# Chunked linear attention and a gated MLP: scores, state and previous output in one tensor-engine visit, a one-sided bounds pass, weight words checked on a second load

## The chip, the cores and the metric

One core of a Trainium2 chip runs one program. The engines are TensorE (PE; its weight loads are PEld), VectorE (DVE), ScalarE (ACT), GpSimd (POOL) and SyncE (SP, which here only issues DMAs). The metric is device time in microseconds. Three executions of the kernel before took 359.44, 359.44 and 360.03 us, median 359.44.

## The reference

Shapes: r, k, v, w are (4 batches, 8 heads, 768 steps, 48), float32; u is (8, 48). The weights are float64 in memory: w_in 384x1024, conv_w 3x1024, w_out 1024x384.

```
state = zeros(B, H, 48, 48)
for t in range(768):
    cur = outer(u * k_t, v_t)
    y_t = r_t @ (state + cur)
    state = w_t[:, None] * state + outer(k_t, v_t)
x = y, heads side by side                  # (4, 768, 384)
h = relu(x @ w_in)                         # (4, 768, 1024)
c = conv_w[0]*h[t-1] + conv_w[1]*h[t] + conv_w[2]*h[t+1]
out = (h * sigmoid(c)) @ w_out             # (4, 768, 384)
```

w lies between 0.80 and 0.95.

## The kernel before

**Attention, by chunks.** The 4 x 768 steps are N = 24 chunks of L = 128 steps, six to a batch. For a chunk, `loads` brings w, k, r, v in (four DMAs on SP). `stage_a` turns w, k, r so that time lies along the free axis (PE transposes, L610), runs two scans over w on DVE (L619 backwards over the chunk, L627 forwards) and multiplies k and r by them (`kr`). The last column of the backward scan is the decay of the whole chunk. Eight heads of 48 rows are packed as six heads plus 16-row pieces of the other two, and `last` holds the pieces put together: from chunk 4 (`EARLY`) on six small SP DMAs per chunk do that (`spread`, L653). `stage_a` also makes the diagonal term (`pm`, POOL and DVE) and turns k back (`kh`, PE L678). Two ACT passes over the loaded w (`guard`, L686, rank put off by `GUARD`) sum what lies above W_HI = 1.05 and below W_LO = 0.75 into `flags`.

`stage_b(n)` is the part around the change, for chunks from 4 on. It works in 64-row and 64-column pieces of the array. One PE operation, "cross" (L872), does three things: `carried(True)`, the carried state's part in the output of chunk n-1 across the two halves (L819); `scores()` of chunk n (L850); `fresh()`, the growth of the state in chunk n (L860). DVE then merges the scores into `pm` (L875), and adds the growth to the decayed state (`sd`, L704 and L707) for `sa` (L880) and `s` (L887). A DVE memset of one element (`mark`, L892) stands between `cross` and the second PE operation, "output" (L897): `carried(False)` (L819) and `within()` (L829) finish the output of chunk n-1 in the banks `ys` that `cross` began. Both must be ordered with DVE between them, as `output` adds to what `cross` wrote from other row groups. ACT and DVE then split the result into two fp32r parts in `xT` (L904, L906), and every few chunks SP copies pieces of it (L915).

**MLP, by blocks.** Eight blocks of 384 steps. In a block each of the 8 column groups of w_in needs nine 128x128 products of 386 columns, in three operations of three (L926); ACT, DVE and POOL make the gate from them (L938 to L948) into `gh` tiles; then each of 3 row tiles needs 24 products with w_out (L955), ACT copies the sum out (L986) and SP stores it.

**Weights.** float64 words are turned into two fp32r parts by `convert` in 9 + 8 pieces (ACT L498, DVE L500 and L503, POOL L506, ACT L520, POOL L521). The words are in a `raw` tile; `small_words` (L512) is then run on the same tile, two ACT passes that overwrite it and sum into `flags` whether a word is too small for the conversion. `raw` and `gh` tiles share a ring of GH = 5 tiles; a raw tile goes back to the ring when its last reader, `small_words`, has ended. There are six such tiles (three of w_in, three of w_out), and conv_w has a small tile of its own.

**Order.** `Plan.op` records every operation with an engine, a modelled length (`LEN`), what it reads and writes and a rank; `Plan.issue` simulates the engines by these lengths, always starts the ready operation of lowest rank, and the instructions are issued in that order, fixed for each engine. `SHIFT` moves ranks by stage and kind. At the end DVE sums `flags`; if it isn't zero, a slow general program runs after the fast one.

Of the kernel before, what the change touches and what calls it, by code (L numbers as in the profile page):

```python
# [18 lines left out]

W_LO, W_HI = 0.75, 1.05  # L20
BANKS = 8
# [6 lines left out]
SPREAD = (3, 5)  # L28
EARLY = 4
COLD = ((9.9, 1.8), (60.0, 1.3))  # L30
CAPS, KEEPS = (3, 4, 4, 3, 4), (1, 3, 1, 1, 1)
# [6 lines left out]
    tr=0.245, kback=0.245, scores=1.0, carried=0.794, state=0.45, y=0.86, state_y=1.22, mm3=0.529,  # L38
    cross=1.16, ends=0.23, half=0.93, output=0.7, cph=0.35, sa=0.27, xhih=0.29, xloh=0.33,
    scan=0.86, small=0.1, pad=0.07, kt=0.47, dg=0.47, cp=0.62, xlo=0.6, sd=0.22, s=0.27,  # L40
    stt=0.54, gate=0.47, wts=0.47, wstt=0.47,
    fill=0.25, kh=0.42, guard=0.72, sbd=0.34, xhi=0.49, relu=0.5, mul=0.49, sig=0.43, cast=0.42, out=0.37, exp=0.52,
    z=0.98, diag=1.07, lo=0.97,
    words=1.15, fetch=1.5, gather=1.6, rest=0.3, carried_rows=1.4, y_rows=1.5, ones=0.8,
    load=0.55, issue=0.45, spread=0.64,
)
SHAPE = dict(cross=3, ends=3, half=3, output=3, scores=1, state=2, y=2, state_y=2, y_rows=2)
TURN = dict(tr=0.18, kback=0.18, carried=0.18)
PAUSE = 0.08
SHIFT = dict(  # L50
    a5=35, a6=61, a8=98, a10=171, a11=-118, a12=44, a15=22, a16=95, a17=160, a20=-37, a23=35, adg=39, agather=-18,
    aguard=56, akback=-108, akh=8, akt=-485, apad=388, asmall=46, aspread=-166, atr=-9, b1=48, b5=-91, b6=20,
    b7=-165, b8=-169, b9=-43, b10=-82, b13=46, b14=-34, b19=-136, b20=20, b21=-5, b24=-21, bcarried_rows=116,
    bcross=-531, bfill=-210, brest=-34, bs=156, bsa=-12, bscores=152, bsmall=43, bxhih=23, bxloh=-10, i0=-56,
    i1=-16, i2=19, i3=44, i4=-25, i5=-15, i6=-84, imm3=-130, icast=27, igate=14, imul=54, istt=-27, l2=33, l4=54,
    l19=12, l20=-2, o1=58, o2=54, o3=300, o4=-43, o5=-9, omm3=37, oissue=15, p0=150, p1=41, p2=-34, p3=-35, p4=-35,
    p5=-17, p6=64, p7=19, p8=168, p10=97, p12=-670, p14=101, pcast=11, pexp=61, plo=-196, pwords=4,
)
# [79 lines left out]
class Plan:  # L138
# [40 lines left out]
    def issue(self):  # L179
# [34 lines left out]
        while len(order) < n:  # L214
            for e in engines:
                if free[e] > t:
                    continue
                for k, (_, i) in enumerate(sorted(ready[e])):
                    if places(self.ops[i][4]):
                        break  # L220
                else:
                    continue
                ready[e].remove((self.ops[i][7], i))
                _, us, _, _, _, moves, port, _ = self.ops[i]
                at = t
                if e == "PE":
                    us *= next((x for until, x in COLD if t < until), 1.0)
                    at = t + self.turn(before, self.what[i])
                    before = self.what[i]
                if port:  # L230
                    other = "POOL" if e == "DVE" else "DVE"
                    at = max(t, locked[other])
                    locked[e] = at + us
                order.append((at, i))
                free[e] = at + us
                if moves:
                    free[e] += wire.add(e, moves, i, free[e])
                else:
                    heapq.heappush(events, (free[e] + TAIL[e], i))
                heapq.heappush(events, (free[e], -1))  # L240
            t = min(wire.next(), events[0][0] if events else float("inf"))
            assert t < float("inf"), "no order found"
            for i in wire.advance(t):
                heapq.heappush(events, (t + (0.8 if self.ops[i][5][2] == 64 else TAIL["SP"]), i))
            todo = []
            while events and events[0][0] <= t + 1e-9:
                todo.append(heapq.heappop(events)[1])
            for i in todo:
                if i < 0:
                    continue  # L250
                for b in self.ops[i][4]:
                    b.uses -= 1
                    if not b.uses:
                        b.kind.held -= 1
                        b.kind.places.append(b.t)
                for u in users[i]:
                    left[u] -= 1
                    if not left[u]:
                        ready[self.ops[u][0]].append((self.ops[u][7], u))
# [87 lines left out]
def rwkv_conv_moe_kernel(  # L347
# [75 lines left out]
    limits = fconst.tile([P, 8], F32, name="limits")  # L423
    guard_lo, guard_hi, small_lo = limits[:, 0:1], limits[:, 1:2], limits[:, 2:4]
    for j, x in enumerate((W_LO, -W_HI, 0x38200000 * 2.0 ** -30, 0x38200000 * 2.0 ** -30 - 2.0)):
# [7 lines left out]
    flags = fconst.tile([P, N + 7, 2], F32, name="flags")  # L433
    nc.vector.memset(flags[:, N:N + 7, :], 0.0)

# [73 lines left out]
    def small_words(raw, buf, k, n, reads, rows=P):  # L509

        for j, kind in enumerate((U32, I32)):
            op("ACT", "words", lambda j=j, kind=kind: nc.scalar.activation(  # L512
                out=raw()[:, 0:2 * n:2].bitcast(F32), in_=raw()[:, 1:2 * n:2].bitcast(kind), func=AF.Relu, scale=-2.0 ** -30,
                bias=small_lo[0:rows, j:j + 1], accum_out=flags[0:rows, N + k, j:j + 1]),
                reads, [buf, ("flag", N + k, j)], rank=plan.rank + GUARD)

# [23 lines left out]
    def win_pieces(m, piece):  # L540
# [9 lines left out]
        for f0 in range(0, DF, HB):  # L550
# [44 lines left out]
    def stage_a(n):  # L595
# [80 lines left out]
        def k_back():  # L676
# [7 lines left out]
            in_=thirds(tb.t).rearrange("p m (g i) -> p g m i", g=2)[:, :, :, D:64]), [tb], [(kh, 1)], [kh])  # L684
        for j, (bias, scale) in enumerate(((guard_hi, 1.0), (guard_lo, -1.0))):
            op("ACT", "guard", lambda j=j, bias=bias, scale=scale: nc.scalar.activation(  # L686
                out=junk.t, in_=W.t[:, :, 0:D], func=AF.Relu, bias=bias, scale=scale, accum_out=flags[:, n, j:j + 1]),
                [W], [junk, ("flag", n, j)], rank=plan.rank + GUARD)

# [9 lines left out]
    def decayed(n):  # L699
# [92 lines left out]
    def stage_b(n):  # L792
# [4 lines left out]
        if out_of is not None:  # L797
# [35 lines left out]
            if qc:  # L833
                own += [q["sd"], (q["sd"], 1)]
            rd += own
            wr += ys
# [28 lines left out]

        def cross():
            if out_of is not None:
                carried(True)
            if new:
# [19 lines left out]
        if out_of is None:  # L889
            return  # L890
        mark = ys[0 if qc else 1]
        op("DVE", "small", lambda: nc.vector.memset(mark.t[0:1, NP * HL:NP * HL + 1], 0.0), [], ys)  # L892

        def output():
            carried(False)
            within()
        op("PE", "output", output, [*own, q["v"], q["pm"], (q["pm"], 0), (q["pm"], 1), (q["pm"], 2)], ys, [q["last"]])  # L897
        slots = slice(KT * qodd, KT * qodd + NP)
# [167 lines left out]
    for n in range(N + 1):  # L1066
# [29 lines left out]
    plan.rank, plan.stage = CHUNK * N, "k"  # L1096
    op("DVE", "small", lambda: nc.vector.tensor_reduce(out=fsum, in_=flags, axis=AX.XY, op=ALU.add),
       [("flag", n, j) for n in range(N + 7) for j in range(2)], ["fsum"])
    op("PE", "small", lambda: nc.tensor.matmul(total.t[0:1, 0:1], lhsT=fsum, rhs=ones_f[:, 0:1], start=True, stop=True),
# [38 lines left out]
```

## Time and profile before

| | |
|---|---|
| median of 3 executions | 359.44 us |
| profiled execution, its own time | 359.42 us |
| span of the trace | 357.7 us |
| mean granted TensorE clock | 0.971 |
| PE busy | 329.7 us (92%) |
| DVE busy | 264.5 us (74%) |
| ACT busy | 238.2 us (67%) |
| POOL busy | 185.2 us (52%) |
| moved by DMA | 34.67 MB |

The span runs from the first to the last instruction. A row of the trace gives an engine, the line of the kernel, the operation, output and inputs by the program's names, shapes and a count; times are microseconds unless a row says ns. Matmuls overlap in the array, so a matmul's duration is longer than its share of the engine, and the distance between starts is what counts. PEclk is the granted clock as a part of full speed.

### The profile page before, as it was taken

Reading aid. Unit: us, or ns where it says so; the run is one execution under the profiler, and the core shown is the slowest. Engines: PE = TensorE matmul, PEld = TensorE weight load, DVE = VectorE, ACT = ScalarE, POOL = GpSimd, SP = SyncE. Lnnn points to the kernel's source line nnn. Section 1 sums busy time; section 2 is a strip of 40 time slices with the busy share of each in tenths; the row PEclk is TensorE's granted clock in tenths of the full one; section 3 lists DMA queues with packets and bytes.
Section 4 is the critical chain, followed back from the end, with each engine's and each line's share of the span. In section 5 each row is a group of like instructions: output and inputs, shape, how many; then the busy total and the mean of one; then the engine's idle time right before and its main releaser. Section 6 shows DMA issues by size and latency. Waiting matters only on the chain.

```text
span 357.7 us, 10946 instructions
## 1 busy us (share of the span) xinstructions
PE 329.7 (92%) x4278; PEld 301.8 (84%) x4278; DVE 264.5 (74%) x596; ACT 238.2 (67%) x638; POOL 185.2 (52%) x243
## 2 busy tenths in 40 slices
PE   6788886789999999999999999899999999999992
PEld 3677775568889889889999999899999899999991
DVE  4579997998988898589988775698979534667400
ACT  5559797999998874687768425778774224777601
POOL 8957778897966462455364431644562210444400
PEclk9889989969999999999999999999999999999998
DMA  8899946533245366434232634633421131000102
GB/s 166 255 274 252 240 108 142 101 76 73 41 81 110 79 123 140 104 66 87 67 79 70 134 92 86 142 85 75 99 53 27 43 92 24 23 23 2 46 26 71
DMA packets 112674, 34.67 MB, mean 97 GB/s; under 512 B 102925, under 2 KB 110630, under 8 KB 112230
## 3 DMA queue, kind: packets, MB, share of 16 engines
q1 hardware_dynamic: 112180, 30.74, 38.5%
q0 software_dynamic: 432, 3.15, 2.3%
q8 instruction: 35, 0.57, 0.7%
q14 instruction: 25, 0.20, 0.2%
q10 hardware_dynamic: 2, 0.00, 0.0%
HBM read 25.19 MB, written 4.72 MB: 84 GB/s over the span
## 4 chain that ended last, share of the span: by engine, by line
PE 67%; DVE 10%; ACT 9%; DMA 5%; POOL 4%; issue 2%; SPq 0%; DVEq 0%; ACTq 0%; POOLq 0%
PE bank L955 25%; PE bank L926 23%; PE bank L610 5%; PE bank L819 3%; DMA r<-in_r_dram 3%; PE bank L829 2%; PE bank L850 2%; DVE a L940 2%; DVE a L942 2%; PE bank L860 2%; PE bank L678 1%; ACT a L944 1%; DVE kr L619 1%; DVE g L945 1%; ACT a L939 1%
## 5 line engine op out<-in xcount | busy, mean ns | idle before, releaser
L926 PE MATMUL bank<-xT,wi 128*128 128x386 f32 x576 | 123.0, 350 | 5.1 <-ACT xT L790 2.3
L955 PE MATMUL bank<-wo,gh 128*128 128x384 f32 x576 | 123.9, 347 | 1.5 <-POOL gh L948 1.4
L926 PEld LDWEIGHTS bank<-xT,wi 128*128 128x128 f32 x576 | 101.0, 191 | 8.5 <-ACT xT L790 2.6
L948 POOL TENSOR_TENSOR gh<-g,gh 128x384 fp32r<-128x384 f32 x64 | 64.3, 1015 | 82.3 <-ACT gh L947 72.3
L955 PEld LDWEIGHTS bank<-wo,gh 128*128 128x128 f32 x576 | 99.2, 188 | 3.5 <-POOL gh L948 2.1
L940 DVE SCALAR_TENSOR_TENSOR a<-bank,cw,a 128x384 f32<-128x384 f32 x64 | 38.2, 609 | 17.9 <-ACT a L939 17.6
L938 ACT ACTIVATE bank<-bank 128x386 f32<-128x386 f32 x64 | 30.8, 481 | 20.0 <-PE bank L926 19.4
L670 POOL TENSOR_SCALAR_AFFINE_SELECT pm<-dg 64x512 f32<-64x512 f32 x40 | 26.3, 658 | 32.1 <-PE bank L829 30.8
L945 DVE TENSOR_TENSOR g<-bank,a 128x384 f32<-128x384 f32 x64 | 34.6, 549 | 7.4 <-ACT a L944 6.8
L947 ACT CAST gh<-g 128x384 fp32r<-128x384 f32 x64 | 32.0, 510 | 9.7 <-DVE g L945 7.9
L942 DVE SCALAR_TENSOR_TENSOR a<-bank,cw,a 128x384 f32<-128x384 f32 x64 | 38.2, 607 | 0.3
L944 ACT ACTIVATE a<-a 128x384 f32<-128x384 f32 x64 | 32.8, 521 | 8.1 <-DVE a L942 7.8
L939 ACT ACTIVATE a<-bank,cw 128x384 f32<-128x384 f32 x64 | 36.0, 578 | 0.3
L657 POOL TENSOR_TENSOR z<-r,k 128x384 f32<-128x384 f32 x24 | 24.3, 1013 | 22.9 <-DMA r<-in_r_dram 13.4
L686 ACT ACTIVATE junk<-w,limits 128x384 bf16<-128x384 f32 x48 | 29.5, 615 | 0.6 <-PE bank L391 0.4
L619 DVE TENSOR_TENSOR_SCAN kr<-bank,one_end 128x387 f32<-128x387 f32 x24 | 23.0, 957 | 6.8 <-POOL kr L458 4.0
L659 POOL TENSOR_TENSOR z<-z,ubc 128x384 f32<-128x384 f32 x24 | 24.3, 1011 | 1.5
L986 ACT COPY wide<-bank 128x384 f32<-128x384 f32 x24 | 11.5, 478 | 17.7 <-PE bank L955 17.3
L627 DVE TENSOR_TENSOR_SCAN kr<-bank,dA 128x387 f32<-128x387 f32 x24 | 22.9, 955 | 0.3
L904 ACT CAST xT<-bank 112x256 fp32r<-112x256 f32 x40 | 13.3, 380 | 13.7 <-PE bank L829 13.7
L506 POOL TENSOR_TENSOR wide<-wide,wide 128x384 int32<-128x384 int32 (+2 forms) x18 | 16.7, 931 | 7.7 <-DVE wide L503 5.0
L906 DVE TENSOR_TENSOR xT<-bank,xT 112x256 fp32r<-112x256 f32 x40 | 15.2, 414 | 6.8 <-ACT xT L904 6.7
(131 smaller groups left out, 575.4 us busy)
## 6 DMA issues: line engine op xcount, KB each, us to landing
w<-in_w_dram SPq DMA_DIRECT2D x24, 192.0 KB, 3.4
k<-in_k_dram SPq DMA_DIRECT2D x24, 192.0 KB, 3.3
r<-in_r_dram SPq DMA_DIRECT2D x24, 192.0 KB, 3.2
v<-in_v_dram SPq DMA_DIRECT2D x24, 192.0 KB, 3.1
out_dram<-wide SPq DMA_DIRECT2D x24, 192.0 KB, 2.1
gh<-in_moe_w_out_dram SPq DMA_DIRECT2D x2, 1152.0 KB, 6.9
last<-kr SPq DMA_DIRECT2D x120, 16.2 KB, 1.9
xT<-xT SPq DMA_DIRECT2D x18, 64.0 KB, 3.2
```

The source lines that it names most:

```text
L619: op("DVE", "scan", lambda: nc.vector.tensor_tensor_scan(out=kr.t[:, 0, WID - 1:0:-1], data0=wp.t[:, WID - 1:0:-1], data1=one_end[:, WID - ...
L686: op("ACT", "guard", lambda j=j, bias=bias, scale=scale: nc.scalar.activation(out=junk.t, in_=W.t[:, :, 0:D], func=AF.Relu, bias=bias, sca ...
L926: nc.tensor.matmul(t.t[:, 0:HB + 2], lhsT=wi[:, m, a, f * P:(f + 1) * P], rhs=xT[:, x0 + m, c, xs], start=(m == 0 and j == 0), stop=(m == ...
L938: ("ACT", "relu", lambda: nc.scalar.activation(out=h(0, width + 2), in_=h(0, width + 2), func=AF.Relu), [t], [t]),
L939: ("ACT", "mul", lambda: nc.scalar.mul(out=a(), in_=h(1), mul=cw[:, 1, bass.ds(f, 1)]), [t, "cw"], [a1]),
L940: ("DVE", "stt", lambda: nc.vector.scalar_tensor_tensor(out=a(), in0=h(0), scalar=cw[:, 0, bass.ds(f, 1)], in1=a(), op0=ALU.mult, op1=ALU. ...
L942: ("DVE", "stt", lambda: nc.vector.scalar_tensor_tensor(out=a(), in0=h(2), scalar=cw[:, 2, bass.ds(f, 1)], in1=a(), op0=ALU.mult, op1=ALU. ...
L944: ("ACT", "sig", lambda: nc.scalar.activation(out=a(), in_=a(), func=AF.Sigmoid), [], [a1]),
L945: ("DVE", "gate", lambda: nc.vector.tensor_tensor(out=g.t[:, 0:width], in0=h(1), in1=a(), op=ALU.mult), [t, a1], [g]),
L947: ("ACT", "cast", lambda: nc.scalar.copy(out=part(0)[:, 0:width], in_=g.t[:, 0:width]), [g], [key]),
L948: ("POOL", "lo", lambda: nc.gpsimd.tensor_tensor(out=part(1)[:, 0:width], in0=g.t[:, 0:width], in1=part(0)[:, 0:width].bitcast(F32), op=AL ...
L955: nc.tensor.matmul(acc.t[:, 0:DM], lhsT=part(a)[:, tt * P:(tt + 1) * P], rhs=wo[:, f, c, :], start=(f == 0 and a + c == 0), stop=(f == FT ...
```

## The change

- `stage_b`: the one operation "cross" becomes three: "cross" (only `carried(True)`, but it waits for all that the three read), "half" (`scores` and `fresh` of chunk n) and "output" (`carried(False)` and `within` of chunk n-1). "half" and the memset `mark` have ranks 30 and 60 below that of "cross", "output" 60 below. The memset is recorded right behind "cross".
- `Plan.issue`: in the model an operation of PE that depends on another of PE may start when that one's issue ends, without the tail `TAIL["PE"]`.
- `guard`: one ACT pass per chunk, for w below W_LO. The upper bound is dropped; in its place DVE takes the maximum of the chunk's decays (`top`, 128x3 to 128x1), and at the end checks that none is above 1.
- `small_words` no longer runs on the tiles that are converted. `again(k)`, at chunks 10, 12, ... 20, takes a tile of the ring, loads the same words again by a DMA issued on ACT's queue, and runs the two ACT passes on that.
- `decayed`: the decayed state of the pieced heads is made by ACT ("sdl", a scaled copy) instead of DVE (L707).
- `LEN` and `SHIFT` have other numbers, so the order of all engines is made anew.

```diff
-W_LO, W_HI = 0.75, 1.05
+W_LO = 0.75
+AGAIN = 10
+NEXT = 30.0
...
+                    if e == "PE":
+                        heapq.heappush(events, (free[e], -2 - i))
...
+                soon, i = i < 0, max(i, -2 - i)
...
                 for u in users[i]:
+                    if soon != (self.ops[i][0] == "PE" == self.ops[u][0]):
+                        continue
...
-        small_words(lambda: row()[:, 0:2 * DF], raw, m, DF, [(raw, 0)])
...
-        small_words(lambda: raw.t[:, 0:n, :].rearrange("p t c -> p (t c)"), raw, KT + t0 // 3, n * DM, [(raw, 0)])
+    def again(k):
+        raw, n = Buf(raw_k), DF if k < KT else min(3, FT - 3 * (k - KT)) * DM
...
+        op("ACT", "issue", lambda: nc.scalar.dma_start(out=rows(), in_=source), [], [(raw, 0)], [raw], moves=(0.0027 * n, 1.0, 8))
+        small_words(words, raw, k, n, [(raw, 0)])
...
-        for j, (bias, scale) in enumerate(((guard_hi, 1.0), (guard_lo, -1.0))):
-            op("ACT", "guard", ...)
+        op("ACT", "guard", lambda: nc.scalar.activation(
+            out=junk.t, in_=W.t[:, :, 0:D], func=AF.Relu, bias=guard_lo, scale=-1.0, accum_out=flags[:, n:n + 1]),
+            [W], [junk, ("flag", n)], rank=plan.rank + GUARD)
+        op("DVE", "top", lambda: nc.vector.tensor_reduce(out=top[:, n:n + 1], in_=kr.t[:, 0, 1:WID:SL], axis=AX.X, op=ALU.max),
+           [kr], [("top", n)], rank=plan.rank + GUARD)
...
-        op("DVE", "small", lambda: nc.vector.tensor_scalar(
-            out=sd.t[:, KT, 0:D], in0=old.t[:, KT], scalar1=last.t[:, 0, 1:2], scalar2=None, op0=ALU.mult),
-            [old, *lasts(n)], [(sd, 1)], [sd, last], port=True)
+        op("ACT", "sdl", lambda: nc.scalar.mul(out=sd.t[:, KT, 0:D], in_=old.t[:, KT], mul=last.t[:, 0, 1:2]),
+           [old, *lasts(n)], [(sd, 1)], [sd, last])
...
-        op("PE", "cross" if new and out_of is not None else "half" if new else "ends", cross, rd, wr, hold)
+        if out_of is not None:
+            mark = ys[0 if qc else 1]
+            def output():
+                carried(False)
+                within()
+            op("PE", "cross", lambda: carried(True), rd, [*ys, ("crossed", n)], hold + wr)
+            plan.rank = rank - 2 * NEXT
+            op("DVE", "small", lambda: nc.vector.memset(mark.t[0:1, NP * HL:NP * HL + 1], 0.0), [], ys)
+        if new:
+            plan.rank = rank - NEXT if out_of is not None else rank
+            def half():
+                scores()
+                fresh()
+            op("PE", "half", half, rd + [("crossed", n)], sc, hold)
+        if out_of is not None:
+            op("PE", "output", output, own + inner, ys, hold)
...
+        if n >= AGAIN and (n - AGAIN) % 2 == 0 and (n - AGAIN) // 2 < 2 * KT:
+            again((n - AGAIN) // 2)
...
+    op("DVE", "small", lambda: nc.vector.tensor_scalar(out=top, in0=top, scalar1=1.0, scalar2=None, op0=ALU.is_gt),
+       [("top", n) for n in range(N)], ["top"])
```

## Rows read from the trace of the kernel before

**Rows 1.** Page, part 1: busy us, share of the span, instructions.

```profile
PE 329.7 (92%) x4278; PEld 301.8 (84%) x4278; DVE 264.5 (74%) x596; ACT 238.2 (67%) x638; POOL 185.2 (52%) x243
```

**Rows 2.** Busy time by stretch: PE, PEld, DVE, ACT, POOL, clock, DMA share, GB/s.

```profile
40.00:80.00 40.00, 30.92 (x503) 25.70 (x502) 37.61 (x82) 34.66 (x95) 33.91 (x38) 0.89 0.53 118
80.00:340.00 260.00, 256.28 (x3442) 239.97 (x3441) 199.32 (x450) 175.63 (x454) 121.25 (x134) 1.00 0.34 75
```

**Rows 3.** The chain that ended last: start, length, what.

```profile
306.97 1.58 PE bank L955 x9
```

**Rows 4.** PE in order of time around one cross and one output: start, span, what.

```profile
205.08 0.54 PE L850 MATMUL bank<-kr 48*64 48x64 f32 x24
...
205.56 0.66 PE L860 MATMUL bank<-v,kh 64*64 64x48 f32 x32
206.14 1.84 PE L955 MATMUL bank<-wo,gh 128*128 128x384 f32 x9
207.91 0.27 PE L819 MATMUL bank<-kr,sd 48*64 48x64 f32 x1
...
209.39 0.49 PE L610 MATMUL bank<-ident,w 128*128 128x128 f32 x3
209.72 0.49 PE L610 MATMUL bank<-ident,k 128*128 128x128 f32 x3
209.97 2.36 PE L955 MATMUL bank<-wo,gh 128*128 128x384 f32 x12
```

**Rows 5.** All instructions of L860: duration ns min/median/max.

```profile
L860 PE MATMUL bank<-v,kh x640: 202/205/253, 53.8 to 290.8; 64*64 64x48 f32 x84, 64*48 64x48 f32 x76
```

**Rows 6.** DVE and PE around memsets and a PE result: start, span, what.

```profile
64.86 0.06 DVE L892 MEMSET bank<- 1x1 f32 x1
...
64.98 0.27 PE L819 MATMUL bank<-kr,sd 48*64 48x64 f32 x1 [0.27 <-DVE bank L892]
...
290.61 0.40 PE L860 MATMUL bank<-v,kh 64*48 64x48 f32 x11
...
290.98 0.36 DVE L880 TENSOR_TENSOR sa<-bank,sd 112x192 f32<-112x192 f32 x1 [3.00 <-PE bank L860]
```

**Rows 7.** Groups by line: busy us, mean ns, idle before.

```profile
L619 DVE TENSOR_TENSOR_SCAN kr<-bank,one_end 128x387 f32<-128x387 f32 x24 | 23.0, 957 | 6.8 <-POOL kr L458 4.0 <-PE bank L610 2.5
L686 ACT ACTIVATE junk<-w,limits 128x384 bf16<-128x384 f32 x48 | 29.5, 615 | 0.6 <-PE bank L391 0.4
L512 ACT ACTIVATE gh<-gh,limits 128x1024 f32<-128x1024 uint32 (+5 forms) x12 | 15.1, 1258 | 0.0
L624 DVE RECIPROCAL dA<-kr 128x3 f32<-128x3 f32 x24 | 4.2, 175 | 0.4
L729 ACT COPY sbx<-sd 48x48 f32<-48x48 f32 x6 | 1.4, 227 | 0.1
```

**Rows 8.** Waits, all engines: total us, times, longest us.

```profile
DVE a L940 <- ACT a L939: 17.6, 15, 4.3
...
PE bank L819 <- DVE bank L892: 0.3, 1, 0.3
```

**Rows 9.** DVE's L707 by stretch: busy us, clock, DMA share, GB/s.

```profile
40.00:60.00 20.00, 1.22 (x2) 0.91 0.60 145
60.00:80.00 20.00, 0.91 (x1) 0.86 0.47 92
```

**Rows 10.** ACT in order of time on the third w_in tile.

```profile
68.64 0.44 ACT L520 CAST wi<-wide 128x256 fp32r<-128x256 f32 x1
...
79.20 1.27 ACT L512 ACTIVATE gh<-gh,limits 128x1024 f32<-128x1024 int32 x1
```

**Rows 11.** DMA issues: KB each, median us to landing; and L653's own.

```profile
gh<-in_moe_w_out_dram SPq DMA_DIRECT2D x2, 1152.0 KB, 6.9
...
DMA to landing us min/median/max: 1.8/1.9/4.1
```

More of the change, by code (lines that the diff above doesn't have):

```diff
@@ L38 @@
     tr=0.245, kback=0.245, scores=1.0, carried=0.794, state=0.45, y=0.86, state_y=1.22, mm3=0.529,
-    cross=1.16, ends=0.23, half=0.93, output=0.7, cph=0.35, sa=0.27, xhih=0.29, xloh=0.33,
+    cross=0.33, half=1.0, output=0.8, cph=0.35, sa=0.27, xhih=0.28, xloh=0.33,
     scan=0.86, small=0.1, pad=0.07, kt=0.47, dg=0.47, cp=0.62, xlo=0.6, sd=0.22, s=0.27,
     stt=0.54, gate=0.47, wts=0.47, wstt=0.47,
-    fill=0.25, kh=0.42, guard=0.72, sbd=0.34, xhi=0.49, relu=0.5, mul=0.49, sig=0.43, cast=0.42, out=0.37, exp=0.52,
+    fill=0.19, kh=0.37, guard=0.62, sbd=0.34, xhi=0.49, relu=0.41, mul=0.47, sig=0.43, cast=0.41, out=0.37, exp=0.46,
     z=0.98, diag=1.07, lo=0.97,
-    words=1.15, fetch=1.5, gather=1.6, rest=0.3, carried_rows=1.4, y_rows=1.5, ones=0.8,
+    words=1.15, top=0.1, sdl=0.27, fetch=1.5, gather=1.6, rest=0.3, carried_rows=1.4, y_rows=1.5, ones=0.8,
     load=0.55, issue=0.45, spread=0.64,
 )
-SHAPE = dict(cross=3, ends=3, half=3, output=3, scores=1, state=2, y=2, state_y=2, y_rows=2)
+SHAPE = dict(cross=3, half=3, output=3, scores=1, state=2, y=2, state_y=2, y_rows=2)
 TURN = dict(tr=0.18, kback=0.18, carried=0.18)
@@ L248, in issue @@
             for i in todo:
-                if i < 0:
+                if i == -1:
                     continue
-                for b in self.ops[i][4]:
+                soon, i = i < 0, max(i, -2 - i)
+                for b in self.ops[i][4] if not soon else ():
                     b.uses -= 1
@@ L423, in rwkv_conv_moe_kernel @@
     limits = fconst.tile([P, 8], F32, name="limits")
-    guard_lo, guard_hi, small_lo = limits[:, 0:1], limits[:, 1:2], limits[:, 2:4]
-    for j, x in enumerate((W_LO, -W_HI, 0x38200000 * 2.0 ** -30, 0x38200000 * 2.0 ** -30 - 2.0)):
+    guard_lo, small_lo = limits[:, 0:1], limits[:, 1:3]
+    for j, x in enumerate((W_LO, 0x38200000 * 2.0 ** -30, 0x38200000 * 2.0 ** -30 - 2.0)):
         nc.vector.memset(limits[:, j:j + 1], x)
@@ L432, in rwkv_conv_moe_kernel @@
             nc.gpsimd.iota(half[0:D], pattern=[[0, 1]], base=(2 * m + (g if m < 2 else 1 - g)) * D, channel_multiplier=1)
-    flags = fconst.tile([P, N + 7, 2], F32, name="flags")
-    nc.vector.memset(flags[:, N:N + 7, :], 0.0)
+    flags = fconst.tile([P, 2 * N + 14], F32, name="flags")
+    top = flags[:, N + 14:2 * N + 14]
+    nc.vector.memset(flags[:, N:N + 14], 0.0)
     xT = const.tile([P, 2 * KT + 1, 2, SP2], F32R, name="xT")
@@ L564, in wout_pieces, with words @@
             convert(lambda t=t: raw.t[:, t, :], wo[:, t0 + t, 0, :], wo[:, t0 + t, 1, :], DM, [raw, (raw, 0)], ("wo", t0 + t))
-        small_words(lambda: raw.t[:, 0:n, :].rearrange("p t c -> p (t c)"), raw, KT + t0 // 3, n * DM, [(raw, 0)])
+    def again(k):
+        raw, n = Buf(raw_k), DF if k < KT else min(3, FT - 3 * (k - KT)) * DM
+        def words():
+            return raw.t.rearrange("p j c -> p (j c)")[:, 0:2 * n]
+        if k < KT:
+            rows, source = words, w_in[k * P:(k + 1) * P, :]
+        else:
+            t = 3 * (k - KT)
+            rows, source = lambda: raw.t[:, 0:n // DM, :], w_out[t * P:t * P + n // DM * P, :].rearrange("(t p) c -> p t c", p=P)
+        op("ACT", "issue", lambda: nc.scalar.dma_start(out=rows(), in_=source), [], [(raw, 0)], [raw], moves=(0.0027 * n, 1.0, 8))
+        small_words(words, raw, k, n, [(raw, 0)])
     chunks = {}
@@ L834, in stage_b @@
                 own += [q["sd"], (q["sd"], 1)]
-            rd += own
+            inner = [q["v"], q["pm"], (q["pm"], 0), (q["pm"], 1), (q["pm"], 2)]
+            rd += own + inner
             wr += ys
@@ L864, in stage_b @@
             hold.append(last)
[L866 to L869, printed above, removed]
+        rank = plan.rank
+        if out_of is not None:
[9 more added lines that the diff above has]
+            def half():
                 scores()
                 fresh()
-        op("PE", "cross" if new and out_of is not None else "half" if new else "ends", cross, rd, wr, hold)
+            op("PE", "half", half, rd + [("crossed", n)], sc, hold)
+        if out_of is not None:
+            op("PE", "output", output, own + inner, ys, hold)
+        plan.rank = rank
         if new:
@@ L890, in stage_b @@
             return
[L891 to L897, printed above, removed]
         slots = slice(KT * qodd, KT * qodd + NP)
@@ L1087, in rwkv_conv_moe_kernel @@
             stage_b(n)
+        if n >= AGAIN and (n - AGAIN) % 2 == 0 and (n - AGAIN) // 2 < 2 * KT:
+            plan.stage = f"q{(n - AGAIN) // 2}"
+            again((n - AGAIN) // 2)
         while bi < len(blocks) and blocks[bi][0] * NCH + min((blocks[bi][1] + HB) // L, NCH - 1) <= (n if n < EARLY else n - 1):
@@ L1096, in rwkv_conv_moe_kernel @@
     plan.rank, plan.stage = CHUNK * N, "k"
-    op("DVE", "small", lambda: nc.vector.tensor_reduce(out=fsum, in_=flags, axis=AX.XY, op=ALU.add),
-       [("flag", n, j) for n in range(N + 7) for j in range(2)], ["fsum"])
+    op("DVE", "small", lambda: nc.vector.tensor_scalar(out=top, in0=top, scalar1=1.0, scalar2=None, op0=ALU.is_gt),
+       [("top", n) for n in range(N)], ["top"])
+    op("DVE", "small", lambda: nc.vector.tensor_reduce(out=fsum, in_=flags, axis=AX.X, op=ALU.add),
+       ["top", *(("flag", n) for n in range(N + 14))], ["fsum"])
     op("PE", "small", lambda: nc.tensor.matmul(total.t[0:1, 0:1], lhsT=fsum, rhs=ones_f[:, 0:1], start=True, stop=True),
```

21 lines of the change are left out of this document (9 added, 12 removed).

## The prediction

> **What bounds the kernel now.** I read the page's busy times first, then the busy time by stretch, then the chain, and last the order of time on PE. PE is the busiest engine [rows 1], but the share is a mean over two stages. From 80 to 340 us PE is busy 256.28 of 260 us at full granted clock, so 3.7 us in all are idle; nothing else is near (DVE 199.3, ACT 175.6) [rows 2]. In that stage time goes only if PE has less to do. From 40 to 80 us PE is busy 30.92 of 40 us at a mean granted clock of 0.89, DVE 37.61 and ACT 34.66 [rows 2]. There DVE, with ACT close behind, sets the pace, while weights are converted and the first block starts. Up to 9.1 us of idle PE and about 4.4 us of lost clock (40 x 0.11) lie there.
>
> **Part 1, one visit of PE instead of two.** Going from full-array products to 64-row pieces and back costs time on PE. Nine products take 1.58 us where nothing interrupts [rows 3]; the nine between cross and output run from 206.14 to 207.91, that is 1.77 us [rows 4], so going in costs 0.19 us. The 32 matmuls of L860 start at 205.56 and the last ends 0.66 us later; at 0.205 us each [rows 5] the last starts at 206.01, and the next product only at 206.14 [rows 4], so coming out costs 0.13 us less a spacing of 0.015, or 0.12. A merged visit saves one of each: 0.31 us. Chunks 5 to 23 have both parts: 19 x 0.31 = 5.9 us. Chunk 24 has no scores and is not counted.
>
> The visit now has two seams between operations. The trace does not show such seams among small pieces. Nearest: two transposes of separate operations start 0.33 us apart (209.39 to 209.72), against 0.25 us from the second to the product behind it (209.72 to 209.97) [rows 4], so a seam can cost 0.08; between full products of one run it costs nothing. I take 0.05, the nearer to the transposes, as both change operands: 19 x 2 x 0.05 = 1.9. Net -4.0 us; with the ends 0 and 0.08, -5.9 to -2.9.
>
> The memset between cross and output used to lie behind other products: its result was waited for once, 0.3 us [rows 8]. Now only `half` covers it, from 205.08 to 206.01 = 0.93 us [rows 4]. It needs the drain of cross (some 0.2 us, the length of one such matmul), DVE starting as PE ends (290.98 against 290.61 + 0.40 [rows 6]), 0.06 for itself and 0.06 to PE (64.92 to 64.98 [rows 6]): 0.34 us, leaving 0.59 for what DVE has in front. DVE is busy 77% of the stage [rows 2], with instructions of at most 0.957 us (the scan) [rows 7], so a stall of up to 0.37 comes now and then. What waits behind the memset on DVE is the gate's arithmetic, what waits behind output on PE is every product. I take +0.5 us over the run; the ends are 0 and the rival below.
>
> **Part 2, relief of the start.** Removed from ACT before 100 us: the twelve word passes, 15.1 us [rows 7]; and one of two guard passes per chunk (0.615 us each, 24 in all [rows 7]). Added to ACT: a 0.23 us copy per chunk, by the nearest row, L729 [rows 7]. Removed from DVE between 40 and 80: L707, 1.22 + 0.91 = 2.1 us [rows 9]. Added to DVE: `top`, a 128x3 reduction, by the nearest row (a reciprocal of 128x3) 0.175 us [rows 7], four times, 0.7 us. A word pass also holds its tile: the third w_in tile is converted by about 69 us but goes back to the ring only at 80.5, after its words [rows 10]; the ring has five tiles and `gh` needs three per block, so the first block gets a tile some 11 us earlier.
>
> What is that worth? Bounds: 0 (if conversion on DVE is the wall and nothing moves) and 13.5 (all of PE's idle and lost clock). DVE, at 94%, is the nearest row: it loses 2.1 - 0.7 = 1.4 us of work, and its 2.4 us of idle (40 - 37.61) have less to wait for, together 3.8; a little more in the stretches beside it. I take -4.0 us. What is late next is DVE itself. After 100 us fewer guard passes are worth nothing: ACT has 84 of 260 us free, so PE covers them.
>
> **Part 3, the second load.** Six loads of 0.75 to 1.1 MB, 6.2 MB together, go on ACT's queue between chunks 10 and 20, and the twelve passes of about 1.26 us stand there. ACT's free time hides the passes; without that cover the gate, and so `gh`, would be 1.26 us late each time. A load like it takes 6.9 us to land [rows 11]. No load on ACT's queue beside SP's is in the trace of this stage. From one side, 0: the DMA engines are busy 34% there [rows 2]. From the other, the six `spread` copies of a chunk, which PE's visit waits for, land in 1.9 us at the median and 4.1 at the longest [rows 11]: 6 x 2.2 = 13.2 us if each load met a visit with no slack. I take +0.5, near the lower end, as other loads already run beside the copies at the 1.9 us median. The load also takes one ring tile of five for its time; blocks hold three, so one is left over. SP's and POOL's queues issue nothing new.
>
> The Trainium skill, "DMA: Bandwidth & Descriptors", section "Queues, rings and completion order", says that each DMA engine takes turns between queue rows, a packet at a time. By that rule a load on ACT's queue is not put behind SP's copies but shares every engine with them, and it speaks against this part. The longest landing, 4.1 us, agrees with some such sharing; by the rule in full the loads are a rival of their own, below.
>
> **Part 4, the order.** Every instruction is placed anew by other lengths and shifts. After 80 us that can win at most PE's 3.7 idle us, and can lose as much: 0, bounds +3.7 and -3.7.
>
> **Sum.** Own time of the profiled run 359.42 (span 357.7 and 1.7 around it; the median of the runs, 359.44, is the same): 359.4 - 4.0 - 4.0 + 0.5 + 0.5 = 352.4 us. Own range of this case 349 to 355.5.
>
> **Rivals.**
> - *One term only, about 356.* Either the start is walled by DVE and gives 0, or the visits fall apart: if in the model the memset isn't done when `half` ends (a scan of 0.957 us in front of it), PE takes products in between, and output pays its own way in and out as before. For it: DVE at 94% before 80 us [rows 2]. Against: the ACT work that goes is 15 us. 359.4 - 4.0 + 0.5 = 355.9.
> - *More, about 347.* The start gives 7.5 us, as the ring and the clock recover too, and the seams are free: 359.4 - 7.5 - 5.9 + 1.0 = 347.0. For it: half of the 13.5 us would do.
> - *Slower: PE stands at output for the memset.* Place: the seam from half to output. DVE's order is fixed; where the instruction in front of the memset waits for ACT, as L940 does, 17.6 us in 15 waits or 1.17 us each [rows 8], the cover of 0.59 falls short by 0.58; 19 times that is 11.0 us: 359.4 - 8.0 + 0.5 + 11.0 = 362.9. It turns the sign from 0.39 us per visit on (7.5 / 19). Against: PE waited for that memset once in 20 times before [rows 8].
> - *The loads meet the copies.* 13.2 us less some slack of the copies, say half: 352.4 + 6.6 = 359.0, no change; the page on DMA is the rule for it.
>
> **How the numbers follow.** A measurement of this kernel tells about 0.2% from no change. Chances: forecast 0.52, one term only 0.20, more 0.13, slower by the memset 0.09, loads 0.06. Faster: 0.52 + 0.20 + 0.13 = 0.85 less 0.01 for the top of the second case; the loads' case is split, 0.04 same and 0.02 slower. Faster 0.84, same 0.05, slower 0.11. The range reaches from 346 (the case of more) to 358 (the second case with the order's loss); it leaves out the slower one and the ends of the first two.
>
> **What would show it.** Right: in the changed trace L819, L850, L860, L819, L829 follow with no L926 or L955 between in chunks 5 to 23, and PE busy falls by about 4 us after 80 us; DVE and ACT have idle time before 80 us; the 40 to 80 stretch has more PE busy time and a higher granted clock. Wrong: PE waits for the memset in the waits (more than 5 us in all), or for `last` copies during the six loads, or idle PE before 80 us is as long as it was.

## The result, and the profile after

The changed kernel takes 356.6 us, the median of 20 runs (352.1 to 359.3); the kernel before took 359.4 in 20 runs beside it. Executions more than 1.5% above a kernel's fastest are left out of every ratio in this document; the profiled execution of the changed kernel, 358.99 us (span 357.3), is one of these, so its lines are read for places and orders, and sizes are taken from the runs. The ratio is 0.990, 95% interval 0.988 to 0.992, so about 355.8 us, 3.6 less. The forecast was 352.4 with a range of 346 to 358: faster, as said, by about half of the 7.0 us forecast. The time lies just outside the forecast's own range, 349 to 355.5, and on the time of the rival "one term only", 355.9.

Part 1 of the page of the changed kernel, which answers to [rows 1], and two stretches, which answer to [rows 2]:

```profile
PE 327.6 (92%) x4278; PEld 305.3 (85%) x4278; DVE 255.7 (72%) x600; ACT 229.5 (64%) x610; POOL 184.9 (52%) x243
```

```profile
40.00:80.00 40.00, 28.80 (x367) 25.24 (x364) 29.37 (x68) 30.47 (x83) 30.91 (x36) 0.83 0.72 201
80.00:340.00 260.00, 254.94 (x3570) 242.96 (x3569) 196.72 (x461) 174.73 (x445) 120.73 (x133) 0.99 0.38 85
```

From 40 to 80 us DVE is busy 29.37 us of 40, where it was busy 37.61. That is not relief: it ran 68 instructions there instead of 82, and in the same order without the second loads (experiment 1) it is busy 36.06 us. PE did less too, 28.80 us instead of 30.92, at a lower mean granted clock, while the DMA engines are busy 72% instead of 53% and move 201 instead of 118 GB/s. So both engines stood still more than before, where more PE work and a higher clock were among the prediction's signs of being right. The second loads (L584), and all `spread` copies (L673), in the changed kernel (line, queue and operation, ns of one issue min/median/max, first and last start):

```profile
L584 ACTq DMA_DIRECT2D gh<-in_moe_w_in_dram x3: 334/340/363, 46.2 to 57.4; - x3
L584 ACTq DMA_DIRECT2D gh<-in_moe_w_out_dram x3: 374/380/398, 66.3 to 99.4; - x3
```

```profile
L673 SPq DMA_DIRECT2D last<-kr x120: 585/592/1833, 41.7 to 281.3; - x120
...
DMA to landing us min/median/max: 1.8/1.9/6.3
```

The loads stand at 46 to 99 us, in the start, not between chunks 10 and 20. PE's waits, and the chain of waits in order of time from 64 to 75 us:

```profile
PE bank L871 <- DMA last<-kr: 3.8, 1, 3.8
PE bank L839 <- ACT kh L700: 1.9, 1, 1.9
...
PE bank L839 <- DVE bank L896: 1.0, 3, 0.4
```

```profile
66.10 0.59 SPq L673
66.73 5.65 DMA last<-kr
...
72.52 0.44 PE bank L871 x3
73.00 0.64 PE bank L881 x21
...
75.14 2.31 PE bank L953 x9
```

One copy of 16 KB takes 5.65 us to land, and PE's visit stands for it, 3.8 us: the longest single wait of PE in the run, and one that the prediction named as a sign that it is wrong. The three other traces that have these loads in the same place (experiments 2, 4 and 5) have the same wait, 3.7, 3.4 and 3.6 us. The ten copies of this stretch also start late: issuing the chunk load in front of them kept SP 3.95 us, first here, against 0.37 in the same order without the second loads:

```profile
60.71 3.95 SPq L595 DMA_DIRECT2D w<-in_w_dram  x1
64.72 6.47 SPq L673 DMA_DIRECT2D last<-kr  x10
```

```profile
59.05 0.37 SPq L595 DMA_DIRECT2D w<-in_w_dram  x1
```

The visit itself is as the change meant it. PE around a late chunk, which answers to [rows 4]:

```profile
266.47 1.30 PE L953 MATMUL bank<-xT,wi 128*128 128x386 f32 x6
267.70 0.27 PE L839 MATMUL bank<-kr,sa 48*64 48x64 f32 x1
...
267.97 0.54 PE L871 MATMUL bank<-kr 48*64 48x64 f32 x24
268.31 0.33 PE L871 MATMUL bank<-last 48*64 48x64 f32 x8
268.44 0.56 PE L881 MATMUL bank<-v,kh 64*64 64x48 f32 x29
...
269.13 0.66 PE L849 MATMUL bank<-pm,v 64*48 64x64 f32 x29
269.73 0.80 PE L953 MATMUL bank<-xT,wi 128*128 128x386 f32 x3
```

Scores and cross, half, and output follow with no product between. In the start DVE's and ACT's groups (busy us, mean ns, idle before), which answer to [rows 7], show one guard pass per chunk instead of two, and a reduction of 144 ns where 175 were taken. The word passes are as many and as long as before.

```profile
L520 ACT ACTIVATE gh<-gh,limits 128x1024 f32<-128x1024 uint32 (+5 forms) x12 | 15.0, 1257 | 0.0
L705 ACT ACTIVATE junk<-w,limits 128x384 bf16<-128x384 f32 x24 | 14.7, 611 | 12.1 <-DMA w<-in_w_dram 9.6 <-PE bank L398 1.2 <-DMA k<-in_k_dram 1.2
L708 DVE TENSOR_REDUCE flags<-kr 128x1 f32<-128x3 f32 x24 | 3.5, 144 | 1.0 <-DVE g L972 0.7 <-DVE a L967 0.3
```

Nor did most of them leave the start. All word passes on the six weight tiles, of the kernel before, then of the changed one (duration in ns, then first and last start):

```profile
L512 ACT ACTIVATE gh<-gh,limits x12: 990/1267/1414, 27.8 to 96.0; 128x1024 f32<-128x1024 uint32 x3, 128x1024 f32<-128x1024 int32 x3, 128x1152 f32<-128x1152 uint32 x2, 128x1152 f32<-128x1152 int32 x2
```

```profile
L520 ACT ACTIVATE gh<-gh,limits x12: 1002/1252/1411, 55.1 to 109.3; 128x1024 f32<-128x1024 uint32 x3, 128x1024 f32<-128x1024 int32 x3, 128x1152 f32<-128x1152 uint32 x2, 128x1152 f32<-128x1152 int32 x2
```

Nine of the twelve still start before 100 us, and five between 40 and 80 us where there were six. The prediction had taken all twelve out of the start.

### The profile page after: what moved, and what is told of

Read it like the earlier page. It is cut to its first block, busy times and chain, and to the rows that moved or that the text cites. A ratio compares the mean times of both kernels' runs of the same rounds, so it can differ in the third digit from the quotient of the medians.

```text
span 357.3 us, 11005 instructions
## 1 busy us (share of the span) xinstructions
PE 327.6 (92%) x4278; PEld 305.3 (85%) x4278; DVE 255.7 (72%) x600; ACT 229.5 (64%) x610; POOL 184.9 (52%) x243
## 4 chain that ended last, share of the span: by engine, by line
PE 67%; DMA 11%; DVE 8%; POOL 4%; ACT 3%; SPq 3%; issue 2%; ACTq 0%; DVEq 0%; POOLq 0%
PE bank L953 26%; PE bank L982 24%; PE bank L630 4%; DMA k<-in_k_dram 3%; PE bank L839 3%; DMA r<-in_r_dram 3%; PE bank L849 2%; DMA gh<-in_moe_w_in_dram,limits 2%; DVE kr L639 2%; SPq L673 2%; DMA last<-kr 2%; PE bank L871 2%; PE bank L698 1%; PE bank L881 1%; DVE kr L647 1%
## 5 line engine op out<-in xcount | busy, mean ns | idle before, releaser
L982 PE MATMUL bank<-wo,gh 128*128 128x384 f32 x576 | 116.2, 346 | 0.3 <-POOL gh L975 0.3
L953 PE MATMUL bank<-xT,wi 128*128 128x386 f32 x576 | 113.4, 348 | 2.0 <-DVE g L972 2.0
L953 PEld LDWEIGHTS bank<-xT,wi 128*128 128x128 f32 x576 | 102.9, 192 | 3.4 <-DVE g L972 2.5
L967 DVE SCALAR_TENSOR_TENSOR a<-bank,cw,a 128x384 f32<-128x384 f32 x64 | 38.8, 610 | 11.0 <-ACT a L966 10.3
L969 DVE SCALAR_TENSOR_TENSOR a<-bank,cw,a 128x384 f32<-128x384 f32 x64 | 38.8, 610 | 0.6
L966 ACT ACTIVATE a<-bank,cw 128x384 f32<-128x384 f32 x64 | 37.0, 580 | 1.1 <-DVE g L972 0.5
L705 ACT ACTIVATE junk<-w,limits 128x384 bf16<-128x384 f32 x24 | 14.7, 611 | 12.1 <-DMA w<-in_w_dram 9.6
L839 PE MATMUL bank<-kr,sa 48*64 48x64 f32 (+1 forms) x240 | 17.8, 233 | 1.9 <-ACT kh L700 1.9
```

Source lines behind the costliest of these rows:

```text
L839: nc.tensor.matmul(to(h, m, c, w), lhsT=q["sa" if h else "sd"].t[p, m, 0:w], rhs=rt(out_of, m)[p, HL * h:HL * (h + 1)], start=first(h, c), ...
L953: nc.tensor.matmul(t.t[:, 0:HB + 2], lhsT=wi[:, m, a, f * P:(f + 1) * P], rhs=xT[:, x0 + m, c, xs], start=(m == 0 and j == 0), stop=(m == ...
L966: ("ACT", "mul", lambda: nc.scalar.mul(out=a(), in_=h(1), mul=cw[:, 1, bass.ds(f, 1)]), [t, "cw"], [a1]),
L967: ("DVE", "stt", lambda: nc.vector.scalar_tensor_tensor(out=a(), in0=h(0), scalar=cw[:, 0, bass.ds(f, 1)], in1=a(), op0=ALU.mult, op1=ALU. ...
L969: ("DVE", "stt", lambda: nc.vector.scalar_tensor_tensor(out=a(), in0=h(2), scalar=cw[:, 2, bass.ds(f, 1)], in1=a(), op0=ALU.mult, op1=ALU. ...
L982: nc.tensor.matmul(acc.t[:, 0:DM], lhsT=part(a)[:, tt * P:(tt + 1) * P], rhs=wo[:, f, c, :], start=(f == 0 and a + c == 0), stop=(f == FT ...
```

## The experiments

Ratios are to the kernel before on the same chip, with the 95% interval; times are the ratio times 359.44. One kernel measured in two sets gave 0.977 and 0.972, 1.7 us apart, so a difference across sets counts from about 2 us.

**1. No second loads** (`no_second`): the changed kernel with its order on every engine, without the six loads and their twelve passes.

```diff
-            op("ACT", "words", lambda j=j, kind=kind: nc.scalar.activation(
+            op("ACT", "words", lambda j=j, kind=kind: emit and nc.scalar.activation(
...
-        op("ACT", "issue", lambda: nc.scalar.dma_start(out=rows(), in_=source), [], [(raw, 0)], [raw], moves=(0.0027 * n, 1.0, 8))
-        small_words(words, raw, k, n, [(raw, 0)])
+        op("ACT", "issue", lambda: None, [], [(raw, 0)], [raw], moves=(0.0027 * n, 1.0, 8))
+        small_words(words, raw, k, n, [(raw, 0)], emit=False)
```

> The changed kernel in its own order, but the six second loads of the weights and their twelve passes on ACT are left out (the weights' words are not checked). In the trace of the changed kernel these loads go out at 46, 54, 57, 66, 81 and 99 us, in the start, not at chunks 10 to 20 as the prediction had it. Theory A (they take from the start what its relief gave: copies and chunk loads land late, ACT and the ring are held): about 352 us against 355.8, PE's 3.8 us wait for the copies gone, clock in 40 to 80 us back to 0.89 or more. Rival B (the start is walled by conversion and the first loads whatever comes beside it): 355.8, within 0.3%.

Measured: 0.977 (0.974 to 0.980), 351.1 us; in a second set (experiment 11) 0.972 (0.970 to 0.975), 349.4; mean 350.3. The second loads with their passes cost 355.8 - 350.3 = 5.5 us, not 0.5.

**2. The loads without their passes** (`dma_only`): only the `words` passes are left out, the first two and the last line of the edit above; the loads stay.

> The changed kernel in its own order with the six second loads kept and only their twelve ACT passes left out (the words are loaded and not checked). Theory A with the DMA traffic as the cost: about 355.5 us, as the changed kernel, with the copies still landing late. Theory A with ACT's 15 us as the cost: about 352.5. Rival B: 355.8.

Measured: 0.996 (0.993 to 0.999), 358.0 us. Taking 15.0 us of ACT away gained nothing, so it is the loads themselves. They could cost by their traffic or by the ring tile that each holds until it has landed; in this trace no engine's wait ends at one of the six loads, which speaks for the traffic. (Why it came out 2.2 us above the changed kernel is open; the two were timed in different sets.) Two stretches of `no_second`, then of `dma_only`:

```profile
40.00:60.00 20.00, 15.89 (x198) 13.46 (x195) 17.95 (x41) 14.67 (x45) 17.92 (x21) 0.91 0.48 111
60.00:80.00 20.00, 17.77 (x326) 16.61 (x324) 18.11 (x41) 16.19 (x44) 15.59 (x18) 0.91 0.43 86
```

```profile
40.00:60.00 20.00, 15.71 (x198) 13.11 (x196) 17.56 (x40) 14.43 (x45) 17.26 (x20) 0.91 0.83 232
60.00:80.00 20.00, 12.66 (x177) 11.92 (x178) 13.42 (x30) 11.67 (x32) 14.21 (x17) 0.83 0.65 171
```

Until 60 us PE and DVE hardly differ. From 60 to 80 PE loses 5.1 us of work and the mean granted clock falls from 0.91 to 0.83. The first scan of the same two chunks (DVE, start and length) brackets it, first in `no_second`, then in `dma_only`:

```profile
56.43 0.95 DVE L639 TENSOR_TENSOR_SCAN kr<-bank,one_end 128x387 f32<-128x387 f32 x1
...
71.04 0.96 DVE L639 TENSOR_TENSOR_SCAN kr<-bank,one_end 128x387 f32<-128x387 f32 x1 [1.12 <-PE bank L630]
```

```profile
58.00 0.95 DVE L639 TENSOR_TENSOR_SCAN kr<-bank,one_end 128x387 f32<-128x387 f32 x1
...
77.53 0.96 DVE L639 TENSOR_TENSOR_SCAN kr<-bank,one_end 128x387 f32<-128x387 f32 x1
```

14.6 us between them without the loads, 19.5 with them: 4.9 us go in this one stretch. The second trace without the loads (experiment 11) has 14.6 again, the changed kernel 19.8. Of the 4.9, most is PE's wait for `last`. That wait in `no_second`, then in `dma_only`, and the landings of the ten copies (59 to 66 us, then 64 to 71.3; a landing is recorded for only a part of the copies):

```profile
PE bank L871 <- DMA last<-kr: 0.6, 1, 0.6
...
DMA to landing us min/median/max: 1.8/1.8/3.0
```

```profile
PE bank L871 <- DMA last<-kr: 3.7, 1, 3.7
...
DMA to landing us min/median/max: 1.8/4.6/5.6
```

**3. The check of words at the end** (`tail`): the order is the changed kernel's up to about 260 us and is made anew behind it; the second loads come in 14 pieces on SP's queue into tiles that are free by then, and 28 shorter passes stand in the last blocks.

```diff
+    def tail(j):
+        raw, n = (Buf(pm_k), 512) if j < 2 * KT else (Buf(kr_k), DM)
...
+        op("SP", "issue", lambda: nc.sync.dma_start(out=words(), in_=source), [], [(raw, 0)], [raw], moves=(0.0027 * n, 1.0, 8))
+        small_words(words, raw, 7 + j, n, [(raw, 0)], us="words512" if n > DM else "words384")
+    for j in range(2 * KT + FT):
+        plan.rank, plan.stage = CHUNK * N + 40.0, f"z{j}"
+        tail(j)
```

> The changed kernel in its own order up to chunk 23; the second loads come only when the chunks' own tiles are free, from about 270 us on, in fourteen pieces into pm and kr tiles on SP's queue, with twenty-eight shorter ACT passes in the last blocks, where ACT has idle time. All is checked. Theory A (the loads cost 5 us because they fall into the start): 350.5 to 351.5 us. Rival (a second load costs its bytes wherever it goes): 355.8 us.

Measured: 0.979 (0.976 to 0.981), 351.7 us, faster than both kernels. Its load issues and its stretch from 60 to 80 us (the profiled execution took 356.2 us):

```profile
L597 SPq DMA_DIRECT2D kr<-in_moe_w_out_dram x8: 334/377/1270, 262.8 to 294.0; - x8
L597 SPq DMA_DIRECT2D pm<-in_moe_w_in_dram x6: 328/330/383, 280.3 to 301.9; - x6
```

```profile
60.00:80.00 20.00, 17.21 (x227) 16.19 (x231) 18.20 (x40) 15.88 (x42) 15.57 (x19) 0.91 0.45 89
```

At the end the same bytes and the same words cost 1.4 us (351.7 - 350.3, inside what sets differ by), so a second load doesn't cost its bytes wherever it goes. The place is the likely reason, and it isn't tried alone: `tail` also changes the queue, the size of a piece and the tiles.

**4. and 5. Visits parted again** (`split`, `split_all`): the changed kernel with the output moved behind PE's next operation, in the 10 merged visits followed by a product, or in all 18. (Of the 19 visits one had products between cross and half and output already.)

```diff
+        for j in [j for j, (_, i) in enumerate(order) if self.what[i] == "output"]:
+            k = next((k for k in range(j + 1, len(order)) if self.ops[order[k][1]][0] == "PE"), None)
...
+                order.insert(k + 1, order[j])
+                del order[j]
```

> The changed kernel in its own order, but on PE each output operation is moved behind the next operation of three products, so that a visit has products between half and output: 19 extra ways out and in, nothing else moved. If the turn costs the 0.31 us that the trace of before gives: 355.8 + 18 or 19 x 0.31 = 361.5 us. If seams inside the visit and the wait for the memset had eaten the gain (the merge is worth nothing): 355.8.

> As split, but output is moved behind the next full-array operation of any kind, so that all 18 merged visits of the changed kernel are parted (split had parted the 10 that are followed by products, for +2.3 us). If the turn costs 0.23 to 0.31 us: 355.8 + 4.1 to 5.6 = 359.9 to 361.4 us. If the merge is worth only what split showed and no more: 358 us.

Measured: 0.996 (0.994 to 0.998), 358.1 us, and 1.001 (0.998 to 1.003), 359.7 us: 2.3 and 3.9 us above the changed kernel, 0.23 and 0.22 us per visit; all three were timed in different sets. The expected 361.5 for `split` assumed 18 or 19 parted visits and 0.31 us each. The traces point the same way: the fifth and the last of the 20 memsets, in the changed kernel and in `split_all`,

```profile
119.65 0.06 DVE L896 MEMSET bank<- 1x1 f32 x1
...
288.87 0.06 DVE L896 MEMSET bank<- 1x1 f32 x1
```

```profile
116.22 0.06 DVE L902 MEMSET bank<- 1x1 f32 x1
...
287.98 0.06 DVE L902 MEMSET bank<- 1x1 f32 x1
```

lie 169.22 and 171.76 us apart: 2.5 us in 15 visits, 0.17 each. That is little more than chance: the two traces of `no_second`, one kernel, have 170.2 and 168.4 us there. So the sign is likely, and the size is known to about 2 of 3.9 us.

**6. The relief in the old order** (`before_relief`): the kernel before without its fourteen word passes (twelve and two of conv_w) and without one guard pass per chunk, nothing moved. DVE keeps all its work, L707 too, so this tries ACT's part of the relief alone.

```diff
-            op("ACT", "words", lambda j=j, kind=kind: nc.scalar.activation(
+            op("ACT", "words", lambda j=j, kind=kind: None and nc.scalar.activation(
...
-            op("ACT", "guard", lambda j=j, bias=bias, scale=scale: nc.scalar.activation(
+            op("ACT", "guard", lambda j=j, bias=bias, scale=scale: j and nc.scalar.activation(
```

> The kernel before in its own order without the fourteen word passes on ACT and without the pass for the upper bound of w (neither is checked). If the relief of the start is worth what the prediction took for it: 359.4 - 4.0 = 355.4 us or less. If the start is walled by DVE and the loads: 359.4, within 0.3%.

Measured: 0.999 (0.997 to 1.002), 359.2 us: nothing. From 60 to 80 us ACT is busy 14.03 us where it was 18.62, and DVE is the wall that it was (19.30, 19.64 before):

```profile
60.00:80.00 20.00, 14.91 (x302) 11.99 (x303) 19.30 (x43) 14.03 (x39) 17.96 (x21) 0.93 0.46 92
```

**7. to 9. The relief taken back in the new order**, each against `no_second`, whose order they keep: the words checked on the first load, behind the conversion (`words_in_place`); each guard pass run twice (`guard2`); the scaling of the carried state on DVE instead of ACT (`sdl_dve`).

```diff
+                    nc.scalar.activation(
+                        out=words[:, 0:2 * n:2].bitcast(F32), in_=words[:, 1:2 * n:2].bitcast(kind), func=AF.Relu, scale=-2.0 ** -30,
+                        bias=small_lo[:, j:j + 1], accum_out=flags[:, N + 2 * k + j:N + 2 * k + j + 1])
...
+    def twice(**kw):
+        nc.scalar.activation(**kw)
+        nc.scalar.activation(**kw)
...
-        op("ACT", "sdl", lambda: nc.scalar.mul(out=sd.t[:, KT, 0:D], in_=old.t[:, KT], mul=last.t[:, 0, 1:2]),
+        op("ACT", "sdl", lambda: nc.vector.tensor_scalar(
+            out=sd.t[:, KT, 0:D], in0=old.t[:, KT], scalar1=last.t[:, 0, 1:2], scalar2=None, op0=ALU.mult),
```

> The changed kernel in its own order without second loads (as no_second, 350.4 us); the twelve word passes run on ACT on the tile of the first load, right behind its conversion, as in the kernel before, and hold it until they end. All is checked. If the relief of the start is worth the predicted 4 us once the order uses it: 354.4 us. If ACT's passes in the start cost nothing in this order either, as in the kernel before: 350.4 us, within 0.3%.

> The kernel without the second loads (words not checked), order as there, but each guard pass runs twice in a row on ACT, as many passes per chunk as before the change: 24 more passes of about 0.61 us, of which about 8 before 100 us. Theory A (ACT's work in the start is worth time, as 15 us of words in place cost 8.2): those 8 passes, 4.9 us, cost about half, so 353 to 354 us. Theory B (what cost in words in place was the ring tile held 11 us longer, not ACT's time): 350.4 us, ratio 0.976 to 0.978 to the kernel before. After 80 us both expect nothing.

> As no_second (350.4 us), but the decayed state of the pieced heads is made by DVE again, at the same place in the order. If DVE is the wall of the start (the prediction's reading): 1 to 2 us more, 351.4 to 352.4. If DVE has room in this order: 350.4.

Measured: 1.000 (0.997 to 1.002), 359.3 us; 0.987 (0.983 to 0.990), 354.6; 0.983 (0.979 to 0.987), 353.4: 9.0, 4.3 and 3.1 us above `no_second`. So ACT's passes do cost in this order. The guard passes hold no ring tile, so there the ring is not the reason; they do hold the chunk's w tile, so that it is ACT's time alone isn't shown. The 3.1 us for one instruction per chunk on DVE are more than the 1 to 2 expected, and no run tells why. In `words_in_place` ACT is the new wall from 40 to 60 us:

```profile
40.00:60.00 20.00, 15.39 (x152) 13.48 (x151) 14.78 (x32) 19.03 (x56) 14.18 (x16) 0.83 0.46 107
```

19.03 of 20 us, against 14.67 in `no_second`. Where `guard2` loses its 4.3 us isn't settled: the two profiled runs of `no_second` differ by 2.6 us at the first memset (66.4 and 69.0 us) and only 0.3 at the last. Against either, `guard2` loses 1.5 to 3.3 us behind the fifth memset, at 115 us, where the prediction and both expectations had nothing; the same kernel's own spread there is 1.8.

**10. to 12. The memset later** (`mark_late`, then `no_second_b` and `mark_late_b` in one set): `no_second` with each memset one DVE instruction later; 18 of 20 move, the orders of all other engines are the same.

```diff
+        for i in [i for _, i in order if self.what[i] == "mark"]:
+            j = next(j for j, x in enumerate(order) if x[1] == i)
+            k = next(k for k in range(j + 1, len(order)) if self.ops[order[k][1]][0] == "DVE")
...
+            order.insert(min(k, out), x)
```

> The kernel without the second loads (words not checked), and each of the memsets between cross and output stands one instruction later on DVE, behind what followed it (18 of 20 move; mostly gate or scan-sum instructions of some 0.3 to 0.6 us). Theory of the rival 'PE stands at output for the memset': the cover of half is 0.59 us and is used up, so PE waits 0.3 to 0.6 us at each, 5 to 10 us in all: 356 to 360 us. Theory of the forecast (half and DVE's slack cover it, a stall comes now and then): 350.4 to 352 us, PE's waits for that memset 3 to 5 us in all.

> The kernel without the second loads (words not checked) once more, beside the next one on the same chip, since the two were timed at different times before and their profiled runs are 2.0 us apart before the first moved memset has run. All theories: 350.4 us again, within 1 us.

> The memsets one DVE instruction later (words not checked), once more, beside the kernel that it differs from in nothing else. If the 5 us between their medians are the memsets' own: 355 to 356 us again, 4.5 to 5.5 above the other. If only what stands behind the first memset in the profiled runs is theirs (1.5 us) and the rest was one run's start: 351.5 to 352.5.

Measured: 0.990 (0.986 to 0.994) and, in the common set, 0.990 (0.986 to 0.994) against 0.972 (0.970 to 0.975): 356 us, 6.3 us more, 0.35 per memset moved. First and last memset, and PE's waits, of `no_second_b`, then of `mark_late_b`:

```profile
L896 DVE MEMSET bank<- x20: 59/59/59, 69.0 to 282.2; 1x1 f32 x20
...
PE bank L839 <- DVE bank L896: 3.4, 5, 2.0
```

```profile
L904 DVE MEMSET bank<- x20: 59/59/59, 68.1 to 286.4; 1x1 f32 x20
...
PE bank L847 <- DVE bank L904: 7.4, 7, 2.7
```

From 213.2 to 218.3 us between the first and the last, 5.1 more, with 4.0 more of PE's wait for them; in the first trace of `no_second` it is 215.6, so the size is taken from the medians. The rival of the memset is a true mechanism; in the changed kernel's order PE waits only 1.0 us for it.

## Why the prediction was right, and where it was off

In the prediction's own terms the sum was -4.0 (visits), -4.0 + 0.5 (start, memset) and +0.5 (loads). The runs give -3.9, about -5.2, and +5.5: together -3.6. The -5.2 is a remainder, not a measurement of its own, and the other two compare different sets.

- **Visits: right as far as shown.** Net -4.0 forecast, 3.9 in 18 visits by parting them again: 0.31 less two seams of 0.05 is 0.21, and parting cost 0.22 or 0.23. The seams were never seen alone, and parting a visit in a finished order need not cost what merging it gained. The sign named for it, PE's busy time after 80 us falling by 4, was badly chosen: it fell by 1.3, since a fixed stretch holds other work when the start moves.
- **Memset: right in size.** +0.5 forecast; PE waits 1.0 us in all for it in the changed kernel, 3.4 in `no_second`. For the rival's 0.58 per visit, a memset one instruction late costs 0.35. That is under the 0.39 from which it was to turn the sign, but the 0.39 went by a gain of 7.5 us; against the 3.6 that there were, 6.3 us would have made the change slower. So the cover of `half` doesn't hold one more DVE instruction in front of the memset; as far as these runs show, it is the order that the planner wrote that kept the rival away.
- **Relief of the start: not shown to be what was forecast.** "Removed from ACT before 100 us: the twelve word passes" failed in the changed kernel, as nine of them came back with the second loads. `no_second`, which has none, is 9.1 us below the kernel before; less the visits that leaves 5.2 for relief, memset and order together, near the 3.5 forecast for them. But the forecast added up work and idle time as if relief acted in any order, and ACT's part of it is worth 0 in the old one, where DVE is busy 19.30 of 20 us from 60 to 80 (experiment 6): there the prediction's own lower bound held, 0 if DVE is the wall. In the new order the same passes put back cost 4.3 and 9.0. Those two exceed the 5.2 together, so costs of undoing aren't the gains of doing; that an order made without the passes has them in worse places is a guess. How the 5.2 divide between the passes, L707 and the new order stays open, as does the ring tile, which no run tried alone.
- **Second loads: the step that failed.** "Six loads [...] go on ACT's queue between chunks 10 and 20" was read from the chunk at which the diff records them. That isn't when they start. The changed `SHIFT` lowers the rank of these issues by 257 (`qissue`), some twenty chunks of 13, and a rank only chooses among operations that are ready: the fourth load, whose own shift of 277 more than takes that back, still went out at 66 us. With ACT free and a ring tile to be had, the planner issues them, at 46 to 99 us, and their passes with them. The +0.5 was priced for a stage where the DMA engines are busy 34% [rows 2], and they came to one that stood at 53% already. What stood as a rival, the loads meeting the copies, is what happened, at 5.5 us against its 6.6; `dma_only` shows that it's the loads and not their passes, and `tail` that the same bytes need not cost that. The Trainium skill, "DMA: Bandwidth & Descriptors", section "Queues, rings and completion order", lets queues take turns on each engine packet by packet; the copy of 5.65 us against a median of 1.9 agrees with it.
- **The order:** 0 was taken; no run tried it alone.

So the range held while two terms were off in opposite ways: 1.7 us of gain in the start that it didn't count, and 5.0 us of loss that it put at the wrong time. That the time came out within 3.4 us of the forecast is in part luck. It also fell on the rival "one term only" and not for its reasons: 18 of 19 visits stayed merged, and the same order without the second loads takes 350.3.

## What to carry to other kernels

A rank or due time says what goes first among ready work, not when it starts: to predict a moved load, ask when its inputs, its buffer and its queue are free, and price it at that place. A transfer that nothing waits for can still cost when it runs beside small copies that the bottleneck engine waits for; place it where few such copies are due. Before counting relief of an engine as time, ask whether the written order can use it: here ACT's part was worth nothing in the old order, and the new order lost time when it was taken back.

## What the hardware showed that wasn't expected

- With a 1.1 MB load issued on ACT's queue at 66.3 us, a 16 KB copy issued on SP's at 66.7 landed in 5.65 us, where the slowest recorded of the same ten copies without the loads took 3.0. The slowest of the whole run says less: 6.3 with the loads, 4.1 in the kernel before [rows 11], and 4.9 and 5.4 in the two traces of `no_second`.
- SP itself was held: issuing a chunk load took it 3.95 us beside the second loads, 0.37 without them.
- Lost PE work in the start comes with a lower mean granted clock: from 60 to 80 us 0.83 in the changed kernel and in `dma_only`, 0.91 in both traces of `no_second`. The loads are not the only way to it, as `guard2`, without them, has 0.83 there too.
- One 59 ns memset a single DVE instruction later costs 0.35 us, when PE's next 32 pieces wait for it.
